# A recurrent attention and a two-layer product on one core: the first 24 steps take the second product whole in float32

## The chip, the cores and the metric

One core of a Trainium2 chip runs the whole program. The metric is the time of one execution on the device in microseconds. TensorE (PE) multiplies matrices; PEld is its loading of the stationary operand. VectorE (DVE), ScalarE (ACT) and GpSimd (POOL) work on elements; SyncE (SP) issues nearly all DMAs, in order, on one queue. Each engine runs its own instructions in the order in which they are written and waits on semaphores for the others.

## The reference

```python
for t in range(S):                                  # B=4, H=8, S=768, D=48
    cur = np.einsum('bhd,bhe->bhde', u[None] * kt, vt)
    y[:, :, t] = np.einsum('bhd,bhde->bhe', rt, state + cur)
    state = wt[:, :, :, None] * state + np.einsum('bhd,bhe->bhde', kt, vt)
x = y.transpose(0, 2, 1, 3).reshape(B * S, H * D)   # 3072 tokens x 384
h = x @ w_in                                        # 384 x 2048
g = np.maximum(h, 0.0) + alpha * np.minimum(h, 0.0)
out = (g @ w_out).astype(np.float32)                # 2048 x 384
```

The weights `w_in` and `w_out` arrive as 64-bit floats, everything else as 32-bit floats.

## The kernel before

**Tiles.** The tokens go in 24 tiles `q` of 128 (64 time steps of two batch entries). The tiles are put into nine groups of two or three (`GROUPS`), and the 2048 inner columns into 16 weight tiles `j` of 128. A *step* is one group with one weight tile: `moe_up` makes the first product of the group, x times `w_in[j]`, with 256 or 384 columns; ScalarE and VectorE mix it by `alpha` (lines 651 and 653, tile `pos`); `moe_down` multiplies it with `w_out[j]` and sums over `j` in one PSUM bank per token tile, two steps later (`LAG`).

**Parts.** All these products are in three parts. A value is split into a high part (a cast on ScalarE, to the type float32r) and the low rest (a subtraction on VectorE); high times high, low times high and high times low are summed, nine matmuls in `moe_up` (line 645) and three per token tile in `moe_down` (line 666). So a step has a cast and a subtraction of its mixed values (`gh` at line 655, `gl` at 656), and a weight tile has them too (`wh` at 628, `wl` at 630).

**Weights.** `weight_tile(j)` loads the 64-bit words (768 KB, ring `raw` of two) and turns them into 32-bit floats on VectorE: a *clear* (line 619, into `cx`), a *join* (622), an *add* of the low word (625, back into `raw`), after which the high and the low part are made. `raw` is free for the next load when the low *part* (630) has read it.

**Attention.** `prep` makes a tile's decays with two scans and two products on VectorE, `scores` and `outputs` are 64x64 matmuls on TensorE, `take` casts the result to the high part of x and subtracts for the low *rest* (line 547; for the first `LO_BY_PE` tiles TensorE multiplies by minus one and ScalarE copies). From tile `U_BY_PE` on GpSimd makes two products for the term with u (line 401). From tile `EARLY` on the scores of the next tile share a block with the outputs of this one.

**Order.** `PHASES` lists the steps: the first three groups go over weight tiles 0 to 5 one after another, then over 6 to 10, then over 11 to 15, and put their partial sums aside in DRAM (`part`) in between; the other groups go over all 16 at once. `PLACE` and `PLACE_REST` say before which step a tile's attention is due. `Plan.order` then simulates the five engines with the durations written beside each operation and picks, for each engine that is free, the ready operation that is due first. The order that comes out is fixed in the program. Sixteen small operations of two products each (line 709) are there to keep TensorE's clock; they are due last of all.

Of the kernel before, what the change touches and what calls it, by code (L numbers as in the profile page):

```python
# [47 lines left out]
LEAD = 20.0  # L48
# [3 lines left out]
PLACE = {0: (-1, -1), 1: (5, 6), 2: (4, 7, 10)}  # L52
PLACE_REST = (13, 8, 3)
# [3 lines left out]
MADE = 12  # L57
# [3 lines left out]
LO_BY_PE = 2  # L61
SLOW, SLOW_TO = 1.08, 95.0
FILL, FILL_FROM, FILL_GAP = 16, 9.0, 1.0
# [27 lines left out]
class Op:  # L91
    __slots__ = ("eng", "dur", "lat", "fn", "deps", "succ", "due", "lock", "takes", "uses", "kind", "n", "left",
                 "ready", "start", "after")


class Plan:
# [6 lines left out]
    def op(self, eng, dur, fn, r=(), w=(), lat=0.1, due=None, lock=False, kind=None, after=0.0):  # L103
# [3 lines left out]
        o.after = after  # L107
# [26 lines left out]
    def order(self):  # L134
# [14 lines left out]
        ends, lock, dma, mode, now, todo = [], 0.0, 0.0, "M", 0.0, len(ops)  # L149
        for o in ops:  # L150
            o.left, o.ready = len(o.deps), o.after
            if not o.left:
                heapq.heappush(waiting[o.eng], (o.ready, o.n))
        while todo:
# [6 lines left out]
            for e in engines:  # L161
# [28 lines left out]
                o.start, dur, todo = now, o.dur, todo - 1  # L190
# [14 lines left out]
                for s in o.succ:  # L205
                    x = ops[s]
                    x.left -= 1
                    x.ready = max(x.ready, end)
                    if not x.left:
                        heapq.heappush(waiting[x.eng], (x.ready, s))  # L210
# [5 lines left out]
        return sorted(ops, key=lambda o: (o.start, o.n))  # L216


def fast_path(tc, wgt, flag, dmaj, nat, u, ud, vg, wts, alpha, out, part):
# [12 lines left out]
    with tc.tile_pool(name="const", bufs=1) as const, tc.tile_pool(name="psum", bufs=1, space=PSUM) as psum:  # L232
# [28 lines left out]
        r_cx = ring("cx", [P, 2 * DM], 1, I32)  # L261
# [9 lines left out]
        r_pos = ring("pos", [P, GT], 3)  # L271
        r_gh = ring("gh", [P, GT], 3, F32R)
        r_gl = ring("gl", [P, GT], 3, F32R)
# [87 lines left out]
        def prep(q):  # L361
# [4 lines left out]
            if q < U_BY_PE:  # L366
                op("DVE", 0.6, lambda: nc.vector.tensor_tensor(
# [15 lines left out]
            op("DVE", 0.6, lambda: nc.vector.tensor_tensor(
                out=segs(kr, 1), in0=segs(kr, 1), in1=pairs(wv(), SW)[:, :, 0:TK], op=ALU.mult),
               r=[w], w=[(kr, 1)], lock=True)
            op("ACT", 0.15, lambda: nc.scalar.copy(out=pc_all[:, q, :], in_=pairs(suf.ap, SW)[:, :, 1]),
               r=[suf], w=[("pc", q)])

            if q < U_BY_PE:
# [7 lines left out]
                op("ACT", 0.15, lambda: nc.scalar.copy(out=cd.ap.rearrange("p (o a) -> p a o", o=2), in_=pairs(cp.ap[:, 0:H], 2)),  # L397
                   r=[cp], w=[cd])
            else:
# [4 lines left out]
                op("DVE", 0.47, lambda: nc.vector.tensor_reduce(  # L404
                    out=cd.ap, in_=pairs(rk.ap[:, 0:HD], D), axis=AX.X, op=ALU.add), r=[rk], w=[cd])
            for o, ps in ((o, range(i, i + 2)) for o in range(2) for i in (0, 2)):
# [4 lines left out]
                op("ACT", 0.5, diagonal, r=["ident2", cd], w=[(at, o)])  # L411
# [12 lines left out]
        def scores(q):  # L424
# [11 lines left out]
            def rest():  # L436
                for o in range(2):
                    op("DVE", 0.4, lambda o=o: nc.vector.copy_predicated(  # L438
# [4 lines left out]
        def transposes(q):  # L443
# [9 lines left out]
            op("ACT", 0.47, lambda: nc.scalar.copy(out=kn[:, :, 0:R2], in_=pairs(kp.ap[:, 0:NP * R2], R2)), r=[kp], w=["kn"])  # L453
# [3 lines left out]
        def outputs(q, nxt):  # L457
# [68 lines left out]
            def take(last):  # L526


                parts = [(0, (0, 2), lambda i: x.ap[:, i, 0:2, ss], x, 0.35), (1, (0, 1), lambda i: x.ap[:, i, 2, ss], x, 0.25)]
                if last:  # L530
                    parts.append((1, (1, 2), lambda i: xr.ap[:, i, ss], xr, 0.25))
# [26 lines left out]
            else:  # L558
# [14 lines left out]
                t = 0.72 + (0.47 if c > 0 else 0) + (0.47 if up else 0) + (0.47 if sc else 0)  # L573
# [28 lines left out]

        def weight_tile(j):
# [5 lines left out]
            for i0, i1 in ((0, 1), (1, 2)) if j < SPLIT else ((0, 2),):  # L609
# [7 lines left out]
                op("ACT", 0.05 + 0.41 * n, lambda w0=w0: nc.scalar.activation(  # L617
                    out=w0(), in_=w0().bitcast(U32), func=AF.Copy, scale=2.0 ** -29), r=[(raw, 0)], w=[k0])
                op("DVE", 0.1 + 0.22 * n, lambda w1=w1, x=x: nc.vector.tensor_scalar(
                    out=x(), in0=w1(), scalar1=0x07ffffff, scalar2=3, op0=ALU.bitwise_and, op1=ALU.logical_shift_left),  # L620
                   r=[(raw, 0), (raw, 1)], w=[k1, cx], lock=True)
                op("DVE", 0.07 + 0.4 * n, lambda w1=w1, x=x: nc.vector.scalar_tensor_tensor(  # L622
                    out=x(), in0=w1(), scalar=-0x40000000, in1=x(), op0=ALU.bitwise_and, op1=ALU.bitwise_or),
                   r=[k1], w=[cx], lock=True)
                op("DVE", 0.07 + 0.4 * n, lambda x=x, w0=w0, w1=w1: nc.vector.tensor_tensor(  # L625
                    out=w1(), in0=x(), in1=w0(), op=ALU.add), r=[k0, cx], w=[k1], lock=True)
                keys = lambda nm: [(nm, j, i) for i in range(i0, i1)]
                op("ACT", 0.41 * n, lambda w1=w1, hi=hi: nc.scalar.copy(out=hi(), in_=w1().bitcast(F32)),  # L628
                   r=[k1], w=keys("wh"))
                op("DVE", 0.07 + 0.4 * n, lambda w1=w1, hi=hi, lo=lo: nc.vector.tensor_tensor(  # L630
# [4 lines left out]
        def moe_up(n, g, j, lag):  # L635
            x, w = xs[g][0], GROUPS[g] * P
            us = lambda t: t * (0.25 + 0.25 * GROUPS[g])
            hp, pos, gh, gl = (Tensor(r) for r in (bank, r_pos, r_gh, r_gl))
# [374 lines left out]
```

## Time and profile before

| | |
|---|---|
| time, median of 3 runs | 532.82 us (531.82 to 533.63) |
| the profiled execution | 535.27 us, span 533.5 us |
| TensorE matmul, busy | 503.7 us, 94% |
| TensorE weight load, busy | 484.2 us, 91% |
| VectorE, busy | 360.7 us, 68% |
| ScalarE, busy | 306.1 us, 57% |
| GpSimd, busy | 71.1 us, 13% |
| DMA | 78.07 MB, mean 146 GB/s |

The span runs from the first instruction to the last, the time also holds what lies around it. The shares are means over stretches with different limits, so the stretches are looked at one by one below. Lengths of instructions that follow each other overlap by some 0.08 us on VectorE and by more on TensorE, where matmuls are pipelined: the distance from start to start says what one costs.

### The profile page before, as it was taken

The numbers are of one execution on the slowest core, as the hardware profiler recorded it, in microseconds if no ns is written. First come the engines' busy times: TensorE is split into PE (matmuls) and PEld (weight loads), VectorE is DVE, ScalarE is ACT, GpSimd is POOL, SyncE is SP. The second block draws the span as 40 slices with busy tenths as digits, with TensorE's granted clock in tenths as the row PEclk, the third lists the DMA queues.
The fourth block names the chain that finished last, engine by engine and source line by source line (L and its number), as shares of the span: only waits on it lengthen the run. The fifth ranks groups of instructions, "written<-read, shape, count | busy, mean of one in ns | idle before, by whom it ended". The sixth has DMA issues, their size and how long they took to land.

```text
span 533.5 us, 13843 instructions
## 1 busy us (share of the span) xinstructions
PE 503.7 (94%) x5654; PEld 484.2 (91%) x5654; DVE 360.7 (68%) x687; ACT 306.1 (57%) x806; POOL 71.1 (13%) x100
## 2 busy tenths in 40 slices
PE   7976887999999999999999999999999999999993
PEld 7965777999999998999999999999999999999993
DVE  6799889999999986873375666676475444334331
ACT  3755674565746455744656566666676675644441
POOL 2010233400003222040030220120000000000000
PEclk7898898999999999999999999999999999999998
DMA  8656686456726585661253366364544036000101
GB/s 302 201 180 214 215 269 202 142 163 209 253 73 204 154 264 142 196 210 42 47 190 120 104 220 180 114 208 124 156 167 151 29 95 209 9 9 3 43 1 37
DMA packets 31800, 78.07 MB, mean 146 GB/s; under 512 B 4464, under 2 KB 13040, under 8 KB 31728
## 3 DMA queue, kind: packets, MB, share of 16 engines
q1 hardware_dynamic: 31728, 77.10, 45.4%
q8 instruction: 46, 0.75, 0.6%
q14 instruction: 26, 0.21, 0.1%
HBM read 67.45 MB, written 7.47 MB: 140 GB/s over the span
## 4 chain that ended last, share of the span: by engine, by line
PE 77%; DVE 12%; DMA 5%; issue 3%; ACT 1%; SPq 1%; DVEq 0%; ACTq 0%
PE bank L645 34%; PE op L666 33%; PE bank L476 5%; DMA raw<-in_wts_dram 2%; DVE raw L625 2%; PE bank L433 2%; DVE gl L656 1%; DVE wl L630 1%; PE bank L451 1%; DVE pos L653 1%; PE bank L518 1%; DVE suf L371 1%; DVE cx L622 1%; DMA kr<-in_dmaj_dram 1%; DMA part<-os 1%
## 5 line engine op out<-in xcount | busy, mean ns | idle before, releaser
L645 PE MATMUL bank<-x,wh 128*128 128x384 f32 (+1 forms) x864 | 227.2, 324 | 3.1 <-ACT wh L628 3.1
L645 PEld LDWEIGHTS bank<-x,wh 128*128 128x128 f32 x864 | 155.0, 190 | 5.2 <-ACT wh L628 3.8
L645 PE MATMUL bank<-x,wl 128*128 128x384 f32 (+1 forms) x432 | 138.5, 321 | 4.2 <-DVE wl L630 4.2
L666 PE MATMUL op<-wh,gl 128*128 128x384 f32 x384 | 130.2, 339 | 3.2 <-DVE gl L656 3.1
L651 ACT ACTIVATE pos<-bank,alpha_n 128x384 f32<-128x384 f32 (+1 forms) x144 | 78.5, 545 | 93.8 <-PE bank L645 92.6
L666 PE MATMUL op<-wh,gh 128*128 128x384 f32 x384 | 130.7, 340 | 0.8 <-ACT gh L655 0.8
L666 PE MATMUL op<-wl,gh 128*128 128x384 f32 x384 | 129.3, 337 | 0.0
L653 DVE SCALAR_TENSOR_TENSOR pos<-bank,pos 128x384 f32<-128x384 f32 (+1 forms) x144 | 73.0, 507 | 81.5 <-ACT pos L651 81.1
L656 DVE TENSOR_TENSOR gl<-pos,gh 128x384 fp32r<-128x384 f32 (+1 forms) x144 | 81.5, 567 | 48.2 <-ACT gh L655 48.2
L655 ACT CAST gh<-pos 128x384 fp32r<-128x384 f32 (+1 forms) x144 | 68.7, 477 | 64.1 <-DVE pos L653 63.6
L645 PEld LDWEIGHTS bank<-x,wl 128*128 128x128 f32 x432 | 82.2, 190 | 5.0 <-DVE wl L630 5.0
L666 PEld LDWEIGHTS op<-wh,gl 128*128 128x128 f32 x384 | 72.9, 190 | 5.2 <-DVE gl L656 5.0
L666 PEld LDWEIGHTS op<-wh,gh 128*128 128x128 f32 x384 | 72.9, 190 | 2.1 <-ACT gh L655 1.4
L666 PEld LDWEIGHTS op<-wl,gh 128*128 128x128 f32 x384 | 72.8, 190 | 0.0
L419 POOL TENSOR_TENSOR St<-St,pc_all 128x192 f32<-128x192 f32 x44 | 23.7, 558 | 273.0 <-DVE St L583 96.6
L409 ACT ACTIVATE at<-ident,cd 128x64 f32<-128x64 f32 x192 | 51.9, 342 | 2.3 <-PE bank L476 2.1
L401 POOL TENSOR_TENSOR rk<-rk,u_bc 128x384 f32<-128x384 f32 x18 | 21.7, 1206 | 80.5 <-DMA rk<-in_nat_dram 51.7
L371 DVE TENSOR_TENSOR_SCAN suf<-wd,low 128x528 f32<-128x528 f32 x23 | 28.7, 1248 | 4.4 <-DMA wd<-in_dmaj_dram 4.4
L377 DVE TENSOR_TENSOR_SCAN wd<-wd,low 128x528 f32<-128x528 f32 x23 | 31.5, 1368 | 0.2
L438 DVE COPY_PREDICATED at<-mask,bank 128x256 f32<-128x256 int32 x48 | 18.9, 436 | 13.6 <-PE bank L518 9.9
L476 PE MATMUL bank<-at,nv 64*64 64x64 f32 x720 | 20.5, 224 | 3.1 <-issue 1.9
L401 POOL TENSOR_TENSOR rk<-rk 128x384 f32<-128x384 f32 x18 | 22.6, 1258 | 1.3
(97 smaller groups left out, 484.6 us busy)
## 6 DMA issues: line engine op xcount, KB each, us to landing
raw<-in_wts_dram SPq DMA_DIRECT2D x32, 768.0 KB, 4.7
kr<-in_dmaj_dram SPq DMA_DIRECT2D x24, 512.0 KB, 4.3
rk<-in_nat_dram SPq DMA_DIRECT2D x18, 384.0 KB, 4.0
raw<-in_dmaj_dram SPq DMA_DIRECT2D x12, 528.0 KB, 4.1
nv<-in_nat_dram SPq DMA_DIRECT2D x24, 256.0 KB, 4.8
wd<-in_dmaj_dram SPq DMA_DIRECT2D x23, 264.0 KB, 3.5
out_dram<-os SPq DMA_DIRECT2D x46, 96.0 KB, 2.2
part<-os SPq DMA_DIRECT2D x14, 192.0 KB, 4.4
```

Source lines behind the costliest of these rows:

```text
L371: op("DVE", 1.15, lambda: nc.vector.tensor_tensor_scan(out=suf.ap[:, ::-1], data0=wv()[:, ::-1], data1=low[:, ::-1], initial=0.0, op0=ALU. ...
L377: op("DVE", 1.15, lambda: nc.vector.tensor_tensor_scan(out=wv(), data0=wv(), data1=low, initial=0.0, op0=ALU.mult, op1=ALU.max), r=["low"] ...
L401: op("POOL", 1.0, lambda i=i: nc.gpsimd.tensor_tensor(out=rk.ap[:, 0:HD], in0=rk.ap[:, 0:HD], in1=u_bc if i == 0 else rk.ap[:, HD:], op=AL ...
L409: nc.scalar.activation(out=at.ap[:, o, p, :], in_=ident2, func=AF.Copy, scale=cd.ap[:, o * NP + p:o * NP + p + 1])
L419: op("POOL", 0.5, lambda i=i: nc.gpsimd.tensor_tensor(out=St[m][:, i, :, 0:D], in0=St[m][:, i, :, 0:D], in1=pc_all[:, q, i::2].unsqueeze(2 ...
L476: last[0] = nc.tensor.matmul(t.ap[rows, cols], start=(t, rows.start) not in open_, stop=stop, skip_group_check=True, **kw)
L645: nc.tensor.matmul(hp.ap[:, 0:w], lhsT=a[:, j, 0, ks], rhs=x.ap[:, xi, k, 0:w], start=(i == 0), stop=(i == 3 * KT - 1))
L651: op("ACT", us(0.5), lambda: nc.scalar.activation(out=pos.ap[:, 0:w], in_=hp.ap[:, 0:w], func=AF.Relu, scale=alpha_n[:, j:j + 1]), r=[hp, ...
L653: op("DVE", us(0.55), lambda: nc.vector.scalar_tensor_tensor(out=pos.ap[:, 0:w], in0=hp.ap[:, 0:w], scalar=0.0, in1=pos.ap[:, 0:w], op0=AL ...
L655: op("ACT", us(0.41), lambda: nc.scalar.copy(out=gh.ap[:, 0:w], in_=pos.ap[:, 0:w]), r=[pos], w=[gh])
L656: op("DVE", us(0.47), lambda: nc.vector.tensor_tensor(out=gl.ap[:, 0:w], in0=pos.ap[:, 0:w], in1=gh.ap[:, 0:w].bitcast(F32), op=ALU.subtract),
L666: nc.tensor.matmul(ops_[s].ap[:, 0:DM], lhsT=a.ap[:, ts], rhs=w[:, j, 1, :], start=(j == j0 and i == 0), stop=(j == j1 - 1 and i == 2))
```

## The change

- `WHOLE_TO` = 24: in the first 24 steps `moe_down` takes one float32 product of 384 columns per token tile (`whole_products`), of `pos` itself and the whole weight, in place of three. `gh` and `gl` are not made there.
- A weight tile that such a step uses (`whole`, tiles 0 to 12) is added into `cx`, not into `raw`; its first half is parted at once (`parts`), its second half is copied by SyncE from `cx` to `wl` and parted there later, before the first step from 24 on that uses it (`later`). `cx` has two buffers.
- `PHASES`: two groups, not three, share the coming of the weights. With it go `PLACE` and `PLACE_REST`.
- `EARLY` 8 for 10; `LO_BY_PE` 6 for 2; ring `pos` 4 for 3, `gl` 2 for 3.
- The clock-keeping products are `spare`: up to 80, which the planner takes when TensorE has nothing ready before 60 us of its own time. 23 operations come into the order, 16 before; 16 products for 12 open the program.
- The durations written beside the operations change by some per cent; they only move the order.

```diff
-PHASES = [(g, j0, j1) for j0, j1 in ((0, 6), (6, 11), (11, NF)) for g in range(3)] + [(g, 0, NF) for g in range(3, len(GROUPS))]
-EARLY = 10
+PHASES = [(g, j0, j1) for j0, j1 in ((0, 6), (6, 11), (11, NF)) for g in range(2)] + [(g, 0, NF) for g in range(2, len(GROUPS))]
+EARLY = 8
-PLACE = {0: (-1, -1), 1: (5, 6), 2: (4, 7, 10)}
-PLACE_REST = (13, 8, 3)
+PLACE = {0: (-1, -1), 1: (4, 5)}
+PLACE_REST = (12, 7, 3)
-MADE = 12
+WHOLE_TO = 24
+MADE = 16
-LO_BY_PE = 2
+LO_BY_PE = 6
-FILL, FILL_FROM, FILL_GAP = 16, 9.0, 1.0
+FILL, FILL_FROM, FILL_TO = 80, 6.0, 60.0
...
+                if pick is None and e == "PE" and spares and spares[-1].after <= now < FILL_TO and len(bank.free) > 1:
+                    pick = spares.pop()
...
-        r_cx = ring("cx", [P, 2 * DM], 1, I32)
+        r_cx = ring("cx", [P, 2 * DM], 2, I32)
...
+        whole = {j for i, (g, j0, j1) in enumerate(PHASES) for j in range(j0, j1) if begins[i] + j - j0 < WHOLE_TO}
+        later = {}
+        def parts(j, i, cx):
+            h, l = wh[:, j, i], wl[:, j, i]
+            src, keys = (lambda: cx.ap[:, i * DM:(i + 1) * DM].bitcast(F32)), [cx]
+            if i == 1:
+                op("SP", 0.4, lambda: nc.sync.dma_start(out=l.bitcast(I32), in_=cx.ap[:, DM:]), r=[cx], w=[("wl", j, 1)], lat=0.7)
+                src, keys = (lambda: l.bitcast(F32)), [("wl", j, 1)]
+            def split():
+                op("ACT", 0.55, lambda: nc.scalar.copy(out=h, in_=src()), r=keys, w=[("wh", j, i)])
+                op("DVE", 0.58, lambda: nc.vector.tensor_tensor(out=l, in0=src(), in1=h.bitcast(F32), op=ALU.subtract),
+                   r=[*keys, ("wh", j, i)], w=[("wl", j, i)], lock=True)
+            if i == 1:
+                later[j] = split
+            else:
+                split()
...
+                if j in whole:
+                    op("DVE", 0.17 + 0.4 * n, lambda x=x, w0=w0: nc.vector.tensor_tensor(
+                        out=x(), in0=x(), in1=w0(), op=ALU.add), r=[k0], w=[cx], lock=True)
+                    for i in range(i0, i1):
+                        parts(j, i, cx)
+                    continue
...
+            if n < WHOLE_TO:
+                return pos, None
...
+                def whole_products(s=s):
+                    nc.tensor.matmul(ops_[s].ap[:, 0:DM], lhsT=gh.ap[:, s * P:(s + 1) * P], rhs=wl[:, j, 1, :].bitcast(F32),
+                                     start=(j == j0), stop=(j == j1 - 1))
...
+                if n - lag >= WHOLE_TO and j - lag >= j0 and j - lag in later:
+                    later.pop(j - lag)()
```

VectorE before, from the rests of a tile of the third group through the mixings of steps 9 to 11 (`raw` and `cx` hold weights, `St` the state, `cd` the reduction for u, `gl` the low part of a step's values):

```order
L547 TENSOR_TENSOR x_117<-bank_79,x_117 128x128
L547 TENSOR_TENSOR x3s_118<-bank_79,x3s_118 128x128
L653 SCALAR_TENSOR_TENSOR pos_120<-bank_77,pos_120 128x256
L619 TENSOR_SCALAR cx_99<-raw_97 128x768
L630 TENSOR_TENSOR wl<-raw_98,wh 128x768
L656 TENSOR_TENSOR gl_125<-pos_120,gh_122 128x256
L622 SCALAR_TENSOR_TENSOR cx_99<-raw_97,cx_99 128x768
L653 SCALAR_TENSOR_TENSOR pos_121<-bank_78,pos_121 128x256
L583 TENSOR_TENSOR St_93<-bank_76,St_93 128x4x48
L583 TENSOR_TENSOR St_93<-bank_79,St_93 128x4x48
L404 TENSOR_REDUCE cd_111<-rk_105 128x8
L653 SCALAR_TENSOR_TENSOR pos_119<-bank_75,pos_119 128x256
```

VectorE of the change, from the mixing of step 8 through that of step 11 (line 645 is the clear, 648 the join, 652 the add, 622 the part, 685 the mixing, 373 and 383 a product and a scan of the attention):

```order
L685 SCALAR_TENSOR_TENSOR pos_121<-bank_76,pos_121 128x256
L622 TENSOR_TENSOR wl<-cx_99,wh 128x384
L652 ISA cx_100<-raw_97,cx_100 128x1536
L383 SCALAR_TENSOR_TENSOR wd_101<-wd_101,low 128x528
L685 SCALAR_TENSOR_TENSOR pos_122<-bank_79,pos_122 128x256
L645 TENSOR_SCALAR cx_99<-raw_98 128x768
L622 TENSOR_TENSOR wl<-cx_100,wh 128x384
L685 SCALAR_TENSOR_TENSOR pos_123<-bank_75,pos_123 128x256
L648 SCALAR_TENSOR_TENSOR cx_99<-raw_98,cx_99 128x768
L373 TENSOR_TENSOR rk_107<-kr_105 128x512
L652 ISA cx_99<-raw_98,cx_99 128x1536
L685 SCALAR_TENSOR_TENSOR pos_120<-bank_78,pos_120 128x256
```

The rests, the state sums and the reductions of the third group's tiles and every low part of a step are gone from between these steps, and the weights' work stands closer together.

SyncE of the change, while the same weight tiles come (line 633 loads raw weights, 617 copies a second half, 600 moves rows of x, 732 puts partial sums aside):

```order
L633 DMA raw_98<-in_wts_dram 128x1536
L600 DMA x_117<-x3s_119 16x2x256 x6
L633 DMA raw_97<-in_wts_dram 128x1536
L617 DMA wl<-cx_100 128x384
L732 DMA part<-os_129 128x384
L732 DMA part<-os_130 128x384
L633 DMA raw_98<-in_wts_dram 128x1536
L617 DMA wl<-cx_99 128x384
L633 DMA raw_97<-in_wts_dram 128x1536
L617 DMA wl<-cx_100 128x384
```

Each copy into `wl` is new; nine of all thirteen stand directly behind a load of raw weights.

## Rows read from the trace of the kernel before

**Rows 1.** Stretches: length, busy of each engine, granted TensorE clock, DMA share, GB/s

```profile
0.00:24.00 24.00, 20.95 (x311) 19.45 (x312) 16.02 (x26) 12.58 (x45) 4.45 (x22) 0.79 0.80 279
24.00:91.40 67.40, 52.91 (x891) 46.93 (x890) 62.03 (x118) 40.16 (x119) 15.56 (x18) 0.94 0.62 204
91.40:199.20 107.80, 106.81 (x1148) 102.87 (x1148) 101.67 (x190) 62.81 (x151) 18.32 (x22) 0.99 0.58 184
199.20:533.50 334.30, 323.07 (x3309) 314.92 (x3308) 181.02 (x357) 190.53 (x492) 32.73 (x38) 0.99 0.37 113
```

**Rows 2.** Waits of TensorE from 0 to 100 us: total, times, longest

```profile
PE bank L645 <- DVE wl L630: 4.2, 4, 1.4
```

**Rows 3.** VectorE in order of time: start, length, line, operation, out<-in

```profile
27.05 0.42 DVE L653 SCALAR_TENSOR_TENSOR pos<-bank,pos 128x256 f32<-128x256 f32 x1
...
47.93 1.24 DVE L371 TENSOR_TENSOR_SCAN suf<-wd,low 128x528 f32<-128x528 f32 x1
49.10 0.93 DVE L630 TENSOR_TENSOR wl<-raw,wh 128x768 fp32r<-128x768 f32 x1
49.95 0.55 DVE L619 TENSOR_SCALAR cx<-raw 128x768 int32<-128x768 int32 x1
50.41 0.41 DVE L656 TENSOR_TENSOR gl<-pos,gh 128x256 fp32r<-128x256 f32 x1
50.75 0.95 DVE L622 SCALAR_TENSOR_TENSOR cx<-raw,cx 128x768 int32<-128x768 int32 x1
51.62 0.20 DVE L374 RECIPROCAL low<-suf 128x8 f32<-128x8 f32 x1
51.73 0.40 DVE L438 COPY_PREDICATED at<-mask,bank 128x256 f32<-128x256 int32 x1
...
82.77 1.77 DVE L625 CUSTOM_DVE_ANT_0 raw<-raw,cx 128x1536 uint16<-128x1536 uint16 x1
...
94.78 0.55 DVE L653 SCALAR_TENSOR_TENSOR pos<-bank,pos 128x384 f32<-128x384 f32 x1
```

**Rows 4.** GpSimd in order of time, around the add at 82.77

```profile
82.64 1.08 POOL L401 TENSOR_TENSOR rk<-rk 128x384 f32<-128x384 f32 x1
```

**Rows 5.** Waits of VectorE up to 95 us, first and last of those after 27.05

```profile
DVE St L583 <- ACT x3s L536: 1.8, 1, 1.8
...
DVE x L547 <- ACT x L536: 0.5, 1, 0.5
```

**Rows 6.** TensorE in order of time: steps 0, 12 and 48 begin at 24.03, 91.44, 199.01

```profile
24.03 0.36 PE L645 MATMUL bank<-x,wh 128*128 128x256 f32 x1
...
27.28 0.69 PE L433 MATMUL bank<-kr 64*64 64x64 f32 x32 [0.59 <-DVE kr L383]
27.91 2.05 PE L709 MATMUL bank<-os 128*128 128x128 f32 x16
29.72 0.42 PE L666 MATMUL op<-wh,gh 128*128 128x384 f32 x1
...
30.95 0.68 PE L476 MATMUL bank<-nv,kn 64*64 64x48 f32 x32
...
32.84 1.05 PE L394 MATMUL bank<-u_dm,rk 128*128 128x2 f32 x8
33.76 0.58 PE L451 MATMUL bank<-ident,kr 112*128 112x112 f32 x4
...
91.44 0.52 PE L645 MATMUL bank<-x,wh 128*128 128x384 f32 x1
...
199.01 0.33 PE L645 MATMUL bank<-x,wh 128*128 128x384 f32 x1
```

**Rows 7.** The chain of waits, 145 to 150 us: nine matmuls of 384 columns

```profile
147.60 1.56 PE op L666 x9
```

**Rows 8.** Line 689, stores of 192 KB, all of the span

```profile
DMA to landing us min/median/max: 1.9/4.4/5.7
```

**Rows 9.** Line 607, loads of raw weights, 768 KB, 0 to 200 us

```profile
DMA to landing us min/median/max: 4.0/4.3/7.1
```

More of the change, by code (lines that the diff above doesn't have):

```diff
@@ L92 @@
     __slots__ = ("eng", "dur", "lat", "fn", "deps", "succ", "due", "lock", "takes", "uses", "kind", "n", "left",
-                 "ready", "start", "after")
+                 "ready", "start", "after", "spare")
 class Plan:
@@ L101, in __init__, with op @@
         self.ops, self.writer, self.readers = [], {}, {}
-    def op(self, eng, dur, fn, r=(), w=(), lat=0.1, due=None, lock=False, kind=None, after=0.0):
+    def op(self, eng, dur, fn, r=(), w=(), lat=0.1, due=None, lock=False, kind=None, after=0.0,
+           spare=False):
         o = Op()
         o.eng, o.dur, o.lat, o.fn, o.due, o.lock, o.kind = eng, dur, lat, fn, due, lock, kind
-        o.after = after
+        o.after, o.spare = after, spare
         o.n, o.deps, o.succ, o.takes, o.uses, o.start = len(self.ops), {}, [], [], [], None
@@ L132, in op, with order @@
         return o
-    def order(self):
+    def order(self, bank):
         ops = self.ops
@@ L148, in order @@
         ready = {e: [] for e in engines}
-        ends, lock, dma, mode, now, todo = [], 0.0, 0.0, "M", 0.0, len(ops)
+        ends, lock, dma, mode, now = [], 0.0, 0.0, "M", 0.0
+        todo, spares = sum(not o.spare for o in ops), [o for o in reversed(ops) if o.spare]
         for o in ops:
             o.left, o.ready = len(o.deps), o.after
-            if not o.left:
+            if not o.left and not o.spare:
                 heapq.heappush(waiting[o.eng], (o.ready, o.n))
@@ L189, in order @@
                     t.ring.given += 1
-                o.start, dur, todo = now, o.dur, todo - 1
+                o.start, dur, todo = now, o.dur, todo - (not o.spare)
                 if e == "PE":
@@ L208, in order @@
                     x.ready = max(x.ready, end)
-                    if not x.left:
+                    if not x.left and not x.spare:
                         heapq.heappush(waiting[x.eng], (x.ready, s))
@@ L215, in order @@
                 now = min(t for t in times if t > now)
-        return sorted(ops, key=lambda o: (o.start, o.n))
+        return sorted((o for o in ops if o.start is not None), key=lambda o: (o.start, o.n))
 def fast_path(tc, wgt, flag, dmaj, nat, u, ud, vg, wts, alpha, out, part):
@@ L270, in fast_path @@
         r_x3 = ring("x3s", [P, 2, GT], 1, F32R)
-        r_pos = ring("pos", [P, GT], 3)
+        r_pos = ring("pos", [P, GT], 4)
         r_gh = ring("gh", [P, GT], 3, F32R)
-        r_gl = ring("gl", [P, GT], 3, F32R)
+        r_gl = ring("gl", [P, GT], 2, F32R)
         r_os = ring("os", [P, DM], 2)
@@ L396, in prep @@
                 op("PE", 0.9, sums, r=[rk, "u_dm"], w=[cp], kind="MM", due=due_att[q] - 3.5)
-                op("ACT", 0.15, lambda: nc.scalar.copy(out=cd.ap.rearrange("p (o a) -> p a o", o=2), in_=pairs(cp.ap[:, 0:H], 2)),
+                op("ACT", 0.22, lambda: nc.scalar.copy(out=cd.ap.rearrange("p (o a) -> p a o", o=2), in_=pairs(cp.ap[:, 0:H], 2)),
                    r=[cp], w=[cd])
@@ L452, in transposes @@
             op("PE", 0.45, products, r=[(kr, 0), "ident"], w=[kp, "kn"], kind="MM", due=due_att[q] - 3.0)
-            op("ACT", 0.47, lambda: nc.scalar.copy(out=kn[:, :, 0:R2], in_=pairs(kp.ap[:, 0:NP * R2], R2)), r=[kp], w=["kn"])
+            op("ACT", 0.55, lambda: nc.scalar.copy(out=kn[:, :, 0:R2], in_=pairs(kp.ap[:, 0:NP * R2], R2)), r=[kp], w=["kn"])
         xs = {}
@@ L637, in moe_up @@
             us = lambda t: t * (0.25 + 0.25 * GROUPS[g])
-            hp, pos, gh, gl = (Tensor(r) for r in (bank, r_pos, r_gh, r_gl))
+            hp, pos = Tensor(bank), Tensor(r_pos)
             def products():
@@ L667, in products @@
                                          stop=(j == j1 - 1 and i == 2))
+                if gl is None:
+                    op("PE", 0.65, whole_products, r=[gh, ("wl", j, 1)], w=[ops_[s], *([("down", n - lag)] if s == size - 1 else [])],
+                       kind="MM", due=due_step[n] + UNIT * size * (0.5 + (s + 1) / size / 2))
+                    continue
                 op("PE", UNIT / 2, products, r=[gh, gl, ("wh", j, 1), ("wl", j, 1)],
@@ L708, in fill @@
                 for _ in range(2):
-                    nc.tensor.matmul(fl.ap[:, 0:P], lhsT=warm(), rhs=warm(), start=True, stop=True)
-            op("PE", 0.43, fill, r=[(tmp, "warm")], w=[fl], kind="MM", due=1e5, after=FILL_FROM + i * FILL_GAP)
+                    nc.tensor.matmul(fl.ap[:, 0:P], lhsT=ident, rhs=ident, start=True, stop=True)
+            op("PE", 0.43, fill, r=["ident"], w=[fl], kind="MM", after=FILL_FROM, spare=True)
         for q in range(NQ):
@@ L767, in fast_path @@
                 w1 = lambda raw=raw, h=h: raw.ap[:, h * DM:(h + 1) * DM, 1].bitcast(F32)
-                op("ACT", 0.45, lambda w1=w1: nc.scalar.activation(out=w1(), in_=w1(), func=AF.Square), w=[(raw, h)])
-                op("ACT", 0.65, lambda j=j, h=h, w1=w1: nc.scalar.activation(
+                op("ACT", 0.57, lambda w1=w1: nc.scalar.activation(out=w1(), in_=w1(), func=AF.Square), w=[(raw, h)])
+                op("ACT", 0.85, lambda j=j, h=h, w1=w1: nc.scalar.activation(
                     out=w1(), in_=w1(), func=AF.Relu, scale=-1.0, bias=tiny[:, 0:1],
@@ L792, in fast_path @@
         op("DVE", 0.1, lambda: nc.vector.tensor_copy(out=flag, in_=fp.ap[0:1, 0:1]), r=[fp], w=["flag"])
-        order = plan.order()
+        order = plan.order(bank)
         if SHOW:
```

63 lines of the change are left out of this document (32 added, 31 removed).

## The prediction

> **What bounds the kernel now.** I read the stages first, then the waits, then the two engines' own order of time. In [rows 1] the span falls into four stretches, cut at TensorE's first product (24.0), at the first product of step 12 (91.4) and at that of step 48 (199.0) [rows 6]. From 91.4 to 199.2 TensorE is busy 106.8 of 107.8 us and from 199.2 on 323.1 of 334.3 us: there only less TensorE work would help. From 24.0 to 91.4 it is busy 52.9 of 67.4 us at a granted clock of 0.94, and busy flatters it: in those 67.4 us it takes only 12 steps of two token tiles. VectorE is busy 62.0 of the same 67.4 us. The waits say the same: TensorE's longest in the first 100 us is for the low weight parts that VectorE writes [rows 2]. So the kernel has a VectorE-bound stretch of 67 us, in which TensorE loses about 20 us (below), and a TensorE-bound rest. The 535.27 us of the profiled execution are 1.77 us more than its span and 2.45 us above the median of the runs shown (532.82). I sum against the span and carry the difference over to the median. A measurement of this kernel can tell some 0.3% (1.6 us) from no change.
>
> **VectorE from the mixing of step 0 to that of step 12.** These stand at 27.05 and 94.78 [rows 3], 67.7 us apart. I count the instructions between the two in the order of either program and price each by the distance from its start to the next one's [rows 3]: a scan 1.17 (47.93 to 49.10), the part of a whole weight tile 0.85, a clear 0.46, a step's low part (gl) 0.34, a join 0.87. An add goes as a join, a mixing as a gl, the part of half a tile at 0.46 (half of 0.85 and a little), a decay product by its 512 elements of a join's 768 at 0.6, a masked copy at 0.35 (it lasts 0.40 at 51.73, and lengths exceed distances by some 0.08); the rests of the outputs and the state sums, of 128 to 256 elements, at 0.2 to 0.34.
> Before: weights 8 clears, 7 joins, 7 adds, 7 parts, 21.5 us; steps 12 mixings and 12 gl, 8.2; attention 8 scans, 11 products, 10 masked copies, 15 rests, 10 state sums and a few small ones, 28.5. Sum 58.2. Measured 67.7: 5.3 us are six waits [rows 5], and 4.2 us are left, which I put down to instructions that ran longer beside a GpSimd product: an add takes 1.77 us at 82.77 [rows 3] while GpSimd multiplies from 82.64 [rows 4].
> After: 10 clears, 9 joins, 9 adds, 8 parts of half a tile (24 us, though two tiles more are begun, since the second halves are parted later); 12 mixings and no gl (4.1 us, the whole product takes `pos` itself); attention 6 scans, 8 products, 6 masked copies, 4 state sums, 15.8 us: no rests, since TensorE makes those of tiles 2 to 5 now, and nothing of tiles 4 to 6 but one's first product and scan, since they come after step 12, as the order above shows. Sum 43.9.
> Of the contention I leave 1 us, since GpSimd's products begin with tile 6, and keep the waits of 5.3. That is 50.2 against 67.7: **17.5 us earlier** at step 12, which then starts at 73.9. A gain of that size needs TensorE to have room. Its own work from step 0 to 12 after the change, by [rows 6]: 12 first products at two thirds of 1.56 [rows 7], 12.5; 21 whole products at 0.65 (below), 13.7; for tiles 2 and 3 outputs 1.89 each, three score blocks at 0.63, three transposes at 0.5, three sums of 0.92, 10.0; 22 clock-keeping products of 0.23, 5.0; minus products and changes between kinds 2.3. Together 43.5, so it could be at step 12 by 67.5 and has 6 us of room. The same sum for before, with five tiles' attention and 60 parted products, gives 47 of 67.4, hence the loss of 20 us.
>
> **A whole product on TensorE.** Before has no float32 product of 384 columns. A float32 product stands as two records; 16 of 128 columns take 27.91 to 29.72 [rows 6], 0.113 each, so 0.226 a product. Three times that is 0.68. If the records went at the pace of the parted ones (1.56 for nine, [rows 7]) it would be 0.35. The three parted ones that it replaces cost 0.52. I take 0.65, near the float32 row, as a part of 0.113 is fixed: 0.13 more for each of 48 products. 27 of them lie behind step 12, on the path: **+3.5 us** (bounds -4.6 and +4.3).
>
> **What moves behind step 12.** TensorE is the bound there, so each instruction counts. Tiles 4 to 6: outputs 1.89, scores 0.63, transposes 0.5 and about 0.3 for changes of kind, three times, 10.0 us. The sums of tile 5, 0.9. Six minus products of tiles 4 and 5 at the pace of 384 columns in 0.173, 0.5 to 0.8. Two more joined outputs save two changes, -0.6. With the whole products **+14.5 us**. VectorE has by the same count 96 us of work in the 36 steps to step 48 and TensorE 107.6 + 14.5 = 122, so the second halves' parting (13 times 0.46, with ScalarE's copy before it) is covered; without the cover it would be 6 us. From step 48 on nothing changes but places.
>
> **The rest.** Against the granted 0.99 of 91.4 to 199.2 [rows 1] I count -0.9: step 12 begins at half the clock (a matmul lasts 0.52 at 91.44 and 0.33 at 199.01, [rows 6]) behind TensorE's waits, which shrink. More clock-keeping products before step 3 (46 against 32 at 0.113 a record, twice) stand in gaps of the plan: nothing, the value I take, if the gaps are there, 3.2 us if they are none, and below nothing (that 0.9 again) if they keep the clock up. Twelve loads and stores of partial outputs go (two groups' sums, not three's, are put aside), 13 copies of 192 KB from `cx` to `wl` come, on the same queue: nothing by the median landing, 10 us by the longest (rival 3).
> Sum: -17.5 + 14.5 - 0.9 = -3.9 us. The span comes to 529.6 and **the time to 528.9 us**.
>
> **Rivals.**
> 1. TensorE's floor decides: VectorE's waits nearly go, since a step no longer waits for gh and gl, and the whole product is cheap. Step 12 is reached at 68 to 69. 533.5 - 23 + 14.5 - 0.9 gives 524.1 for the span, 523.4 as time. For it: the stretch 91.4 to 199.2, where both engines have 94% and 99% [rows 1] and lose almost nothing. Against: there the work is evenly laid, here the weights come first.
> 2. Nothing is gained: TensorE has 6 us of room now, not 20, so the two engines wait for each other and VectorE's waits double, or the added clock-keeping products stand on the path. Step 12 at 78; span 533.7, time 533.
> 3. Slower, by the copies of `wl`. A whole tile's add writes `cx`, and `cx` (two of them) is cleared for the tile after next only when SyncE's copy of its second half has landed. SyncE issues in order, and a load of raw weights that waits for the same add stands directly ahead of the copy in nine of thirteen cases. The VectorE instructions between an add and the next clear of that buffer take some 5.3 us. A copy of this size landed in 1.9 to 5.7 us, median 4.4 [rows 8], plus 0.3 to issue: just in time. Behind a raw load, which lands in up to 7.1 [rows 9], it would be 7.4, and VectorE would stand 2.1 us. At 1.2 us on each of eight buffers step 12 comes 10 us later: span 539.6, time 538.9. It decides from 0.5 us a tile, which uses up the 3.9. Everything behind on VectorE, the mixings and the scans, waits too. For it: 0.6 us of room by the median. Against: the raw buffer comes free at the add, not at the part, so loads go out earlier.
> The Trainium skill, "DMA: Bandwidth & Descriptors", section "Queues, rings and completion order", says that on each DMA engine the descriptors of one issuing engine's row are taken in ring order. By that rule the copy does stand behind the raw load and rival 3 is the likelier; that a store of 192 KB took 1.9 us at best and 4.4 in the median [rows 8] agrees with it, but shows no copy directly behind a load.
>
> **How the numbers follow.** My forecast has 0.42 (525 to 532: waits of 2 to 8 us, whole products of 0.52 to 0.68), rival 1 0.20, rival 2 0.20, rival 3 0.18. Faster means under 531.2: nearly all of the forecast and rival 1, 0.61. Slower means over 534.4: rival 3 and a little of rival 2, 0.20. The same, 0.19. The range runs from 520, below rival 1 by some of the cheap products' 4 us, to 537, which leaves out most of rival 3's far side.
>
> **What would show it.** Right: step 12's first product (the first on the second run over the first group) between 71 and 77; VectorE over 90% busy up to there with no wait for DMA above 0.5 us; two records of about 0.32 for a whole product; TensorE 98% busy behind step 12 and step 48 at 195 or so. Rival 1 shows step 12 at 69, rival 2 waits of TensorE and VectorE for each other, rival 3 waits of the clear into `cx` for a DMA. If step 48 comes before 190, or the stretch behind it is not 334 us again, the sum is wrong where I believed it safest.

## The result and the profile after

The changed kernel takes 527.32 us (median of 4 runs, 525.84 to 529.0) against 532.81 (4 runs, 531.82 to 533.63): ratio 0.9899, 95% interval 0.9864 to 0.9933. Measured again beside the last experiments, it stands at 0.9864 (0.9833 to 0.9896). It is faster by about 1 to 1.4%.

The four stretches of the changed kernel, cut at the first products of steps 0, 12 and 48 as in [rows 1] (length; busy of TensorE, its weight loads, VectorE, ScalarE, GpSimd; granted clock; DMA share; GB/s):

```profile
0.00:20.93 20.93, 19.50 (x332) 18.15 (x333) 15.89 (x28) 11.90 (x41) 4.44 (x22) 1.00 0.87 309
20.93:74.22 53.29, 46.14 (x528) 36.40 (x526) 45.83 (x77) 31.32 (x84) 5.29 (x6) 0.97 0.73 243
74.22:192.24 118.02, 117.14 (x1488) 104.97 (x1486) 103.40 (x193) 65.82 (x180) 30.03 (x29) 1.00 0.56 173
192.24:527.30 335.06, 323.59 (x3319) 315.84 (x3312) 181.22 (x362) 192.00 (x503) 34.76 (x43) 0.99 0.38 115
```

By the starts in [rows 6], before had 24.03, 67.41, 107.57 and 334.49. The differences are -3.1, -14.1, +10.4 and +0.6: 6.2 us of span. Up to step 12 TensorE is idle 7.2 us instead of 14.5, and behind it 0.9 of 118 us. The starts themselves, TensorE in order of time:

```profile
20.93 0.36 PE L677 MATMUL bank<-x,wh 128*128 128x256 f32 x1
...
69.48 0.58 PE L677 MATMUL bank<-x,wh 128*128 128x256 f32 x1
...
70.85 1.46 PE L699 MATMUL op<-wl,pos 128*128 128x384 f32 x4
71.85 0.58 PE L677 MATMUL bank<-x,wh 128*128 128x256 f32 x1
...
74.22 0.58 PE L677 MATMUL bank<-x,wh 128*128 128x256 f32 x1
...
192.24 0.44 PE L677 MATMUL bank<-x,wh 128*128 128x384 f32 x1
```

Steps 10, 11 and 12 stand 2.37 us apart (L699 is the whole product, two records for each of two tiles). A step of two tiles with parted products, late in the same run, takes 2.11:

```profile
506.02 0.28 PE L677 MATMUL bank<-x,wh 128*128 128x256 f32 x1
...
508.13 0.28 PE L677 MATMUL bank<-x,wh 128*128 128x256 f32 x1
```

So a whole product costs (2.37 - 2.11) / 2 = 0.13 us more, the value that the prediction took. The longest waits in the first 100 us, of TensorE and of VectorE (total, times, longest), answer to [rows 2] and [rows 5]:

```profile
PE op L699 <- DMA wl<-cx: 4.9, 3, 3.7
PE op L699 <- DVE pos L685: 1.2, 1, 1.2
...
DVE suf L377 <- DMA wd<-in_dmaj_dram: 4.5, 1, 4.5
DVE pos L685 <- ACT pos L683: 4.0, 8, 1.0
DVE cx L645 <- DMA wl<-cx: 2.8, 2, 2.3
```

The new waits are for the copy from `cx` to `wl`, on both engines, as rival 3 had it for VectorE. VectorE from the mixing of step 0 to that of step 12, the stretch that the prediction added up, before and after (columns as above):

```profile
27.05:94.78 67.73, 53.60 (x883) 47.81 (x883) 62.39 (x116) 39.46 (x113) 15.46 (x18) 0.92 0.65 217
```

```profile
22.80:76.30 53.50, 46.35 (x522) 36.21 (x522) 45.48 (x77) 32.67 (x86) 5.29 (x6) 0.97 0.73 244
```

VectorE stands idle for 8.0 of these 53.5 us, where it was 5.3 of 67.7 before. The worst single wait is TensorE's in step 2:

```profile
44.45 0.28 PE L677 MATMUL bank<-x,wh 128*128 128x256 f32 x1
48.41 2.90 PE L699 MATMUL op<-wl,pos 128*128 128x384 f32 x4 [3.69 <-DMA wl<-cx]
```

Four records take 2.90 there and 1.46 at 70.85: behind the wait the granted clock is half, the lower of TensorE's two levels, for some 3.4 us (0.57 is the mean of 4 us). The same stretch by windows:

```profile
44.00:48.00 4.00, 0.72 (x7) 0.52 (x5) 3.80 (x6) 0.61 (x2) 0.00 (x0) 1.00 0.50 189
48.00:52.00 4.00, 3.59 (x10) 2.40 (x11) 3.36 (x7) 1.58 (x3) 0.93 (x1) 0.57 0.94 312
52.00:56.00 4.00, 3.30 (x28) 3.08 (x28) 2.71 (x7) 3.60 (x15) 0.64 (x2) 1.00 0.67 239
```

### The profile page after: what moved, and what is told of

Its sections match the earlier page's. It is cut to its first block, busy times and chain, and to the rows that moved or that the text cites. A ratio compares the mean times of both kernels' runs of the same rounds, so it can differ in the third digit from the quotient of the medians.

```text
span 527.3 us, 13761 instructions
## 1 busy us (share of the span) xinstructions
PE 506.4 (96%) x5654; PEld 475.4 (90%) x5654; DVE 346.3 (66%) x657; ACT 301.0 (57%) x806; POOL 74.5 (14%) x100
## 4 chain that ended last, share of the span: by engine, by line
PE 86%; DMA 6%; DVE 4%; issue 1%; ACT 1%; SPq 0%; DVEq 0%
PE bank L677 37%; PE op L705 33%; PE bank L482 6%; PE op L699 5%; DMA wl<-cx 3%; PE bank L439 2%; DMA raw<-in_wts_dram 2%; PE bank L457 1%; PE bank L524 1%; DMA kr<-in_dmaj_dram 1%; DVE suf L377 1%; PE bank L752 1%; DVE wd L383 0%; DVE cx L652 0%; DVE cx L648 0%
## 5 line engine op out<-in xcount | busy, mean ns | idle before, releaser
L705 PE MATMUL op<-wh,gh 128*128 128x384 f32 x336 | 112.9, 336 | 0.7 <-ACT gh L690 0.7
L705 PE MATMUL op<-wh,gl 128*128 128x384 f32 x336 | 112.5, 335 | 0.2 <-DVE gl L691 0.2
L705 PE MATMUL op<-wl,gh 128*128 128x384 f32 x336 | 112.5, 335 | 0.0
L691 DVE TENSOR_TENSOR gl<-pos,gh 128x384 fp32r<-128x384 f32 (+1 forms) x120 | 69.8, 582 | 50.3 <-ACT gh L690 49.3
L690 ACT CAST gh<-pos 128x384 fp32r<-128x384 f32 (+1 forms) x120 | 58.8, 490 | 36.6 <-DVE pos L685 35.9
L705 PEld LDWEIGHTS op<-wh,gh 128*128 128x128 f32 x336 | 63.2, 188 | 1.5 <-ACT gh L690 1.3
L705 PEld LDWEIGHTS op<-wh,gl 128*128 128x128 f32 x336 | 63.2, 188 | 0.7 <-DVE gl L691 0.7
L705 PEld LDWEIGHTS op<-wl,gh 128*128 128x128 f32 x336 | 63.1, 188 | 0.0
L699 PE MATMUL op<-wl,pos 128*128 128x384 f32 x96 | 37.3, 508 | 6.1 <-DMA wl<-cx 4.9
L407 POOL TENSOR_TENSOR rk<-rk,u_bc 128x384 f32<-128x384 f32 x18 | 21.3, 1185 | 122.5 <-DMA rk<-in_nat_dram 118.4
L699 PEld LDWEIGHTS op<-wl,pos 128*128 128x128 f32 x96 | 16.8, 195 | 14.0 <-DVE kr L389 3.9
```

The source lines that it names most:

```text
L690: op("ACT", us(0.54), lambda: nc.scalar.copy(out=gh.ap[:, 0:w], in_=pos.ap[:, 0:w]), r=[pos], w=[gh])
L691: op("DVE", us(0.6), lambda: nc.vector.tensor_tensor(out=gl.ap[:, 0:w], in0=pos.ap[:, 0:w], in1=gh.ap[:, 0:w].bitcast(F32), op=ALU.subtrac ...
L699: nc.tensor.matmul(ops_[s].ap[:, 0:DM], lhsT=gh.ap[:, s * P:(s + 1) * P], rhs=wl[:, j, 1, :].bitcast(F32), start=(j == j0), stop=(j == j1 ...
L705: nc.tensor.matmul(ops_[s].ap[:, 0:DM], lhsT=a.ap[:, ts], rhs=w[:, j, 1, :], start=(j == j0 and i == 0), stop=(j == j1 - 1 and i == 2))
```

## The experiments

In these runs the kernel before had medians of 534.5 to 535.7 (529.9 to 539.1), so I compare ratios to it. "Mixing of step n" is VectorE's instruction of that step: in the changed kernel step 0 mixes at 22.8, 12 at 76.3 and 48 at 194.7; before at 27.05, 94.78 [rows 3] and 202.7. A single edit here also makes the planner lay a new order, so each kernel's profile has to say where its time went.

**The clock-keeping products alone, in the kernel before.**

```diff
-MADE = 12
+MADE = 16
...
-FILL, FILL_FROM, FILL_GAP = 16, 9.0, 1.0
+FILL, FILL_FROM, FILL_TO = 80, 6.0, 60.0
...
```

Left out are the lines of the planner that take the spare products, the same as in the changed kernel.

> The kernel before with the new clock-keeping products alone (16 at the start, spare ones in the plan's gaps). Theory: the first 21 us then run at full clock, VectorE no longer waits 3.6 us for TensorE there, step 0 begins at 21 in place of 24.0, and since VectorE bounds what follows, the 3 us stay: 529.5 to 530.5 us. Rival (what starts earlier is taken back by the coming of the weights): step 0 at 21, but 532 to 533 us.

Measured: 534.82, ratio 1.0005 (0.9976 to 1.0035). In its profile steps 0, 12 and 48 mix at 23.8, 87.3 and 196.0, earlier than before, and the end comes at 530.2, but this was the fastest of its twelve executions (531.95 us); the median shows nothing of it. The run also settles a rival for the gain. The mean granted clock of an execution is 0.989 in the median here, 0.979 in the kernel before, measured beside it, and 0.988 to 0.994 in the changed kernel; since the time here is that of before, a higher clock alone doesn't make the 1%.

**The changed kernel with the clock-keeping products of before** (the same lines the other way).

> The changed kernel with the clock-keeping products of before (12 at the start, 16 small operations due last). Theory: clock of the first 21 us about 0.8, step 0 at 24, and 3 us more: 530 to 531 us. Rival (step 0 is earlier because of VectorE's new order): step 0 at 21 to 22, 527 to 528 us.

Measured: 529.42, ratio 0.9887 (0.9836 to 0.9938); steps 0, 12 and 48 mix at 23.4, 76.0 and 194.3. That is the changed kernel. By the profile the theory fell, since step 0 comes as early; the time lies between theory and rival, and six runs don't part them. Taken with the run above, these products bring nothing that could be measured.

**Parted products throughout, all else as changed.**

```diff
-WHOLE_TO = 24
+WHOLE_TO = 0
```

> The changed kernel with WHOLE_TO = 0: all second products parted, no copies into wl. Theory: VectorE gets 12 low parts at 0.34 and 0.39 more for each of 8 weight parts back, 7.2 us in the stretch to step 12; no waits of the clear into cx (2.8 us less); TensorE gets 27 times 0.13 = 3.5 us back behind step 12: 527.3 + 7.2 - 2.8 - 3.5, 528 to 530 us, step 12 at 78 to 79. Rival (the grouping does it all, the whole product is a loss on TensorE): 524 to 526 us.

Measured: 545.83, ratio 1.0211 (1.0172 to 1.0249). Both expectations fell. TensorE, in order of time:

```profile
64.04 0.34 PE L705 MATMUL op<-wl,gh 128*128 128x384 f32 x1
72.71 1.87 PE L400 MATMUL bank<-u_dm,rk 128*128 128x2 f32 x8 [8.33 <-DVE rk L373]
```

The planner had put four weight tiles ahead of tile 3's attention on VectorE; step 6 mixes at 85.6 instead of 62.6. So this run holds an ill order besides the loss of the whole products.

**Parted products in a better order.** The second products are parted throughout again, and one entry of the planner's places differs besides:

```diff
-WHOLE_TO = 24
+WHOLE_TO = 0
-PLACE = {0: (-1, -1), 1: (4, 5)}
+PLACE = {0: (-1, -1), 1: (3, 4)}
```

> The parted kernel of before's second product in two groups (no whole products, as in the run with 545.8), but the two attentions of group 1 placed a step earlier (after steps 3 and 4 instead of 4 and 5), which puts three fewer weight tiles ahead of step 6 on VectorE: its priced instructions up to step 12 come to 67.7 us instead of 80.7 (61.4 in the changed kernel, 77.0 in the kernel before). Theory (the whole product's own relief is those 6 us, and the rest of the loss of 545.8 was an order that the planner made worse): step 12 mixes at 82 to 84, time 529 to 532. Rival (without whole products the weights come too late in any order, since each whole tile costs VectorE 0.85 more ahead of its step): step 12 at 90 or later, time 535 to 545.

Measured: 536.98, ratio 1.0064 (1.0028 to 1.0101). Step 12 mixes at 77.1, as in the changed kernel: neither the theory's 82 to 84 nor the rival's 90. The time lies in the rival's range, but it is lost behind step 12. The stretch from 76.5 to 125 us, first the changed kernel, then this one:

```profile
76.50:125.00 48.50, 48.17 (x599) 39.28 (x598) 43.84 (x79) 31.33 (x87) 17.58 (x16) 1.00 0.75 245
```

```profile
76.50:125.00 48.50, 38.02 (x337) 34.01 (x336) 46.14 (x74) 29.20 (x72) 16.63 (x14) 0.93 0.62 204
```

TensorE idles 10.5 us instead of 0.3, with VectorE 95% busy. Without whole products the VectorE-bound stretch goes on to 125 us.

**Whole products up to step 12, and up to step 18** (`WHOLE_TO = 12`, `WHOLE_TO = 18`).

> The changed kernel with whole products up to step 12 instead of 24; up to there VectorE's order is the same for a few places. Theory (behind step 12 TensorE is the bound and a whole product costs 0.13 us more than three parted ones): step 12 at 74 as before, 24 whole products fewer behind it, time 527.3 - 24 x 0.13 = 524.2 (523 to 525.5). Rival (behind step 12 VectorE has no room for the parting of whole tiles and the gl of 12 steps): waits of TensorE for wl or gl behind step 12, time 528 to 531.

> The changed kernel with whole products up to step 18 instead of 24: 12 whole products less, 36 parted ones more, 12 low parts (gl) and part of the second halves back on VectorE between steps 18 and 24. Theory (VectorE's relief is needed up to some 125 us, the time of step 28 or so): 12 x 0.5 = 6 us more VectorE work there against 12 x 0.13 = 1.6 less on TensorE, time 529 to 532. Rival (the relief is needed only up to step 18, when the weights are in): 527.3 - 1.6 = 525.7 (525 to 526.5).

Measured: 534.03, ratio 0.9985 (0.9955 to 1.0014), and 532.22, ratio 0.994 (0.9917 to 0.9962): the rival of the first and the theory of the second are what happened, the first at a higher price (534 where 528 to 531 was said). Fewer of the dearer products behind step 12 make the kernel slower, in both cases. Step 12 mixes at 77.0 and 77.6, as it should; from 76.5 to 125, up to step 12 and up to step 18:

```profile
76.50:125.00 48.50, 42.21 (x484) 36.96 (x483) 44.31 (x78) 31.54 (x82) 12.74 (x12) 0.96 0.66 227
```

```profile
76.50:125.00 48.50, 44.38 (x501) 38.03 (x500) 43.60 (x77) 29.76 (x79) 8.71 (x11) 1.00 0.63 205
```

TensorE idles 6.3 and 4.1 us, in the first mostly in waits for `gl` (2.4 us), `gh` (1.4) and `wl` (1.3). The relief of VectorE is needed up to some 125 us, well behind step 18, which mixes at 93.5 in the changed kernel.

**Whole products up to step 32** (`WHOLE_TO = 32`).

> The changed kernel with whole products up to step 32 instead of 24: 16 whole products in place of 48 parted ones, in steps where TensorE is the bound. Theory (0.13 us each): step 48 comes 2.1 us later, time 529.4 (528.5 to 530.5). Rival (VectorE still holds the path between step 12 and 24 and the 8 gl fewer give something back): time 526.5 to 528.

Measured: 529.74, ratio 0.9916 (0.9886 to 0.9945), span 528.7. Against the changed kernel's 0.9899 and 0.9864 that is 0.9 to 2.8 us more, beside the 2.1 worked out; the intervals overlap, so it doesn't decide. In the profiles steps 12 and 48 mix 119.5 us apart, 118.4 in the changed kernel: 1.1 us more, half of the 2.1.

**Three groups share the weights' coming, as before.** `PHASES` and the places as before, the rest as changed.

```diff
-PHASES = [(g, j0, j1) for j0, j1 in ((0, 6), (6, 11), (11, NF)) for g in range(2)] + [(g, 0, NF) for g in range(2, len(GROUPS))]
+PHASES = [(g, j0, j1) for j0, j1 in ((0, 6), (6, 11), (11, NF)) for g in range(3)] + [(g, 0, NF) for g in range(3, len(GROUPS))]
...
-PLACE = {0: (-1, -1), 1: (4, 5)}
-PLACE_REST = (12, 7, 3)
+PLACE = {0: (-1, -1), 1: (5, 6), 2: (4, 7, 10)}
+PLACE_REST = (13, 8, 3)
```

> The changed kernel with three groups sharing the weights, and their places, as before. Theory: the attention of the third group comes back before step 12 (12.7 us of VectorE less 4 us of rests that TensorE keeps), so step 12 comes 9 to 10 us later, at 83 to 84; behind it TensorE has 10 us less: the same within 2 us, 526 to 529 us. Rival (the grouping is what gains): 531 to 533 us.

Measured: 539.08, ratio 1.0093 (1.0055 to 1.013). Step 12 mixes at 99.4 and step 48 at 203.7, 9 us later than in the changed kernel. Up to the mixing of step 12 VectorE is busy 84.3 us here and 63.2 in the changed kernel:

```profile
0.00:99.44 99.44, 87.49 (x1312) 74.70 (x1313) 84.25 (x139) 58.20 (x182) 26.97 (x45) 0.98 0.77 264
```

```profile
0.00:76.30 76.30, 67.72 (x868) 56.23 (x869) 63.23 (x108) 45.04 (x128) 9.73 (x28) 0.98 0.76 259
```

The rival is nearer, and too mild. In the orders tried, whole products without the two groups are slower than the kernel before, and so are two groups without whole products: there each needs the other. The three groups were tried in one order only, so what of the loss is that order's stays open.

**The rests of two tiles instead of six by TensorE** (`LO_BY_PE = 2`).

> The changed kernel with LO_BY_PE back at 2: TensorE makes the rests of the outputs of two tiles instead of six by products with minus one, so 12 minus products leave TensorE and 12 subtractions of rests come back to VectorE, all of them within the first 125 us. Theory (the runs before: from step 12 to some 125 us VectorE still holds the path by little, as the kernels with more VectorE work there fell behind): 12 x 0.27 = 3.2 us more on VectorE, most of it on the path, against 2 us less on TensorE: time 528 to 531. Rival (my prediction: behind step 12 TensorE alone counts and VectorE has cover): 12 x 0.17 = 2 us less, time 525 to 526.

Measured: 532.12, ratio 0.9953 (0.9923 to 0.9984). The time lies a little above the theory's, but not by its cause: from 76.5 to 125 TensorE is busy 47.27 of 48.5 us. Step 12 mixes at 82.0, 5.7 us late, which is more than the whole loss. The wait for the copy came to 4.1 us here, and the granted clock stayed at half behind it for some 16 us:

```profile
44.00:48.00 4.00, 1.06 (x4) 0.31 (x2) 3.25 (x6) 0.49 (x2) 0.00 (x0) 1.00 0.75 238
48.00:52.00 4.00, 2.82 (x6) 1.64 (x6) 2.86 (x4) 2.22 (x4) 0.00 (x0) 0.55 0.53 178
52.00:56.00 4.00, 3.74 (x18) 3.49 (x16) 2.21 (x4) 1.24 (x5) 0.00 (x0) 0.50 0.44 145
56.00:60.00 4.00, 2.98 (x6) 1.52 (x6) 3.32 (x6) 2.61 (x7) 0.00 (x0) 0.50 0.47 177
60.00:64.00 4.00, 3.38 (x17) 3.03 (x16) 1.26 (x4) 1.57 (x4) 1.02 (x2) 0.50 0.91 290
```

That this made step 12 late is likely, not shown: with whole products up to step 12 and with ScalarE's copy (below) the clock stood at half for some 10 us at the same place, and step 12 was only 0.7 and 2.4 us late. What the 12 products are worth is not shown either.

**The copy issued by ScalarE.**

```diff
-op("SP", 0.4, lambda: nc.sync.dma_start(out=l.bitcast(I32), in_=cx.ap[:, DM:]), r=[cx], w=[("wl", j, 1)], lat=0.7)
+op("SP", 0.4, lambda: nc.scalar.dma_start(out=l.bitcast(I32), in_=cx.ap[:, DM:]), r=[cx], w=[("wl", j, 1)], lat=0.7)
```

> The changed kernel with its 13 copies of 192 KB from cx to wl issued by ScalarE instead of SyncE; the order of TensorE and of VectorE is the same, word for word. Theory (the remains of rival 3 are the ring's: a copy stands behind the raw load that SyncE issued just ahead of it): the copies land in 2 to 3 us in the median instead of 4.8, the waits of the clear for the copy (2.8 us in all in the changed kernel) and of the whole product for it (4.9 us) go, step 12 comes 3 to 5 us earlier, time 523 to 525. Rival (the copies are late because the 16 DMA engines are shared with the load, whichever engine issues them, or because the data are needed late anyway): landing over 4 us in the median, waits as before, time 526 to 529.

Measured: 529.83, ratio 0.9935 (0.9902 to 0.9968). The copy of step 2 goes out with the loads and lands no sooner (ScalarE's queue, then SyncE's, then TensorE):

```profile
42.59 0.47 ACTq L617 DMA_DIRECT2D wl<-cx  x1
...
42.58 5.69 SPq L633 DMA_DIRECT2D raw<-in_wts_dram  x2
...
49.91 2.90 PE L699 MATMUL op<-wl,pos 128*128 128x384 f32 x4 [4.14 <-DMA wl<-cx]
```

The median from issue to landing is 5.3 us, 4.8 in the changed kernel. The rival held (the time stands 0.8 us above its range): another queue doesn't help.

**The copy ahead of the load on SyncE's queue**, nine pairs exchanged after the planning (`takes_raw` marks a raw load, `copies` a copy), every other engine's order untouched:

```diff
...
+sp = [i for i, o in enumerate(order) if o.eng == "SP"]
+for i, k in zip(sp, sp[1:]):
+    if hasattr(order[i], "takes_raw") and hasattr(order[k], "copies") and order[k].start - order[i].start < 1.0:
+        order.insert(k, order.pop(i))
```

> The changed kernel with nine neighbours on SyncE's queue exchanged: where a raw weight load of 768 KB stands directly ahead of a copy of 192 KB from cx to wl, the copy is issued first. TensorE, VectorE and ScalarE keep their order, word for word. In the changed kernel TensorE waits 3.7 us for such a copy at 44.7 us, and is granted half its clock for some 4 us behind it; where ScalarE issued the copy at the same moment as SyncE the load, the wait was 4.1 us. Theory (the copy is late because its bytes stand behind or among those of a load that was issued no later): it lands in 2 to 3 us, TensorE's wait at 44.7 falls under 1 us, the clock stays at 1.00 and step 12 mixes at 72 to 73.5 instead of 76: ratio 0.979 to 0.984 to the kernel before, 521.5 to 524 us. Rival (the loads, now 0.5 us later each, are what VectorE waits for next): waits of the clear for the raw load of 3 us or more, ratio as the changed kernel's (0.986 to 0.990).

Measured: 530.45, ratio 0.9899 (0.9859 to 0.994), as the changed kernel. Landing of the copies, and then VectorE's longest wait in the first 100 us:

```profile
DMA to landing us min/median/max: 2.1/2.6/7.2
```

```profile
DVE cx L647 <- DMA raw<-in_wts_dram: 6.8, 5, 2.1
```

In the changed kernel these were 4.8 in the median, and 0.6 us for the raw loads. Both mechanisms are there: the copies land sooner, VectorE's waits for them are gone, and the raw loads, issued some 0.6 us behind a copy each, are waited for instead. TensorE still waits 2.0 us for the copy of step 2, and the clock did not stay at full (0.83 and 0.74 from 40 to 48 us, 0.61 from 52 to 56). Step 12 mixes at 76.3 either way. From 36 to 44 us the DMA engines are full, here at 353 and 410 GB/s:

```profile
36.00:40.00 4.00, 3.89 (x109) 3.21 (x109) 3.18 (x6) 2.88 (x8) 0.00 (x0) 1.00 0.97 353
40.00:44.00 4.00, 2.00 (x5) 0.97 (x4) 2.99 (x5) 0.51 (x1) 0.00 (x0) 0.83 1.02 410
```

No kernel beat the changed one by more than its interval.

**The changed kernel once more.**

> The changed kernel once more, beside the two others on the same chip, so that their differences of 0.3 to 1% are taken from runs of the same hour: ratio 0.986 to 0.993 to the kernel before, as measured first.

Measured: 527.83, ratio 0.9864 (0.9833 to 0.9896), span 525.4.

## Why the prediction was right

The forecast of 528.9 stands 1.6 us above the measured 527.3. The mechanism held: the time up to step 12, where VectorE is the bound, fell by more than TensorE's work behind it rose. That step 12 came at 74.2 where 73.9 was said is luck: it began 3.1 us earlier and gained 3.4 us less. In the span the terms missed by -3.1, +3.4, -3.2 and +0.6 us, which leaves -2.3.

- **-17.5 up to step 12: too much.** The stretch became 14.1 us shorter. The count of VectorE's work held: 43.9 and 1 us of contention were forecast between the two mixings, and it is busy 45.5. "Keep the waits" did not hold: it is idle 8.0 us there, not 5.3, and 2.8 of these are the clear's waits for the copy. TensorE itself waits 4.9 us for the copies in the first 100 us, a place that the sum left out, and runs some 3.4 us at half its clock behind the longest. "VectorE over 90% busy" was wrong too: it is 86%.
- **Nothing at the start: missed.** Step 0 came 3.1 us earlier. The granted clock is 1.00 there instead of 0.79 [rows 1]. It is 1.00 as well in the changed kernel with before's clock-keeping products and in the kernel before with the new ones, so neither these products nor the new order is needed for it; why the one trace of the kernel before has 0.79 stays open. In the kernel before an earlier start brought nothing to the timed runs.
- **+14.5 behind step 12, with -0.9 for the clock: 3.2 too much.** The whole products' 0.13 us was right. The term that was too large is "tiles 4 to 6, three times": by the two traces two blocks of scores, two of transposes and 2.33 of outputs move behind step 12, not three of each, which takes off 0.63 + 0.5 + 0.67 x 1.89 = 2.4 us.
- **"Covered" on VectorE: true of this kernel, by a hair.** The prediction compared 96 with 122 us up to step 48; VectorE was busy 103.4 of 118.0. Its work is not evenly laid in that time: up to 125 us it is 90% busy, and the kernels with whole products up to 12 or 18 show that what they add there comes out as TensorE's idle time.
- **Rival 3 was half there.** The wait of the clear for the copy is 2.8 us in all, not 1.2 on each of eight buffers; the copy took 4.8 us in the median (5.1 when the changed kernel was run again), near its 4.4 [rows 8]. "No wait for DMA above 0.5 us" failed. The Trainium skill, "DMA: Bandwidth & Descriptors", section "Queues, rings and completion order", has a row's descriptors taken in ring order; the exchange on SyncE's queue agrees (2.6 against 4.8 us). The same section lets each DMA engine take turns between rows, but lets a transfer's semaphore increment land only after every earlier write of that engine, across its queues. So it doesn't say that a copy on a row of its own is done ahead of a load, and here it landed in 5.3 us, which agrees; no run shows which of the two decides.
- **Rival 1** needed VectorE's waits to go; they grew to 8.0 us. **Rival 2** needs step 12 at 78; it came at 74.2.

What makes the gain is shown by undoing, as far as the orders tried go (0.988 is the middle of the changed kernel's two ratios): without whole products +1.9% (the better of two orders; 1.0064 / 0.988), without the two groups +2.2% (one order; 1.0093 / 0.988). The clock-keeping products give nothing that could be measured; the second buffer of `cx`, `EARLY`, the rings and the changed durations were not undone. Both effective parts relieve VectorE in the first 125 us, which the prediction named, though it ended that stretch at step 12.

## What to carry to other kernels

A dearer product on TensorE can pay even where TensorE is the bound on average, as long as the other engine holds the path: look for the time at which it lets go by windows of both engines, not at a step's start. When one number feeds a planner, undo an edit in at least two orders, or the order's harm is booked to the edit (1.0211 against 1.0064). A copy that is late behind a load can be let ahead of it, but here the load was then what was waited for.

## What the hardware showed

Behind a wait of TensorE of 3 to 4 us between 44 and 50 us, the granted clock was half for some 3.4 us in the changed kernel (wait 3.7), for some 10 in two others (3.1 with whole products up to step 12, 4.1 with ScalarE's copy) and for some 16 with `LO_BY_PE = 2` (4.1). Step 12 mixed at 76.3, 77.0, 78.7 and 82.0 us there. What decides how long the clock stays down, and how much of the lateness is the clock's, no run shows. A copy of 192 KB within the chip landed in 2.1 to 8.3 us. Where nine of the thirteen stood behind a load on the same queue the median was 4.8 and 5.1 (two executions), on ScalarE's queue 5.3, ahead of the load 2.6.
